# Batch 0's opening rearranged: a preload in 16 transfers, A normalised in two parts, the vote's values in PSUM, first w1 in fewer transfers

## The chip, the cores and the metric

One program on one core of a Trainium2 chip. The metric is the device time of one execution in microseconds. Three runs of the kernel before took 450.25, 451.38 and 451.59 us; their median, 451.38 us, is the time to beat.

## What is computed

Two stages in one program, with B=8 batches, H=8 heads, S=576 tokens, D=64; the model width is 512, there are E=8 experts of F=1024.

```python
# attention with 32 landmarks (means over 18 tokens), per batch and head
A  = softmax(q @ k_lm.T / 8)      # 576 x 32
Bm = softmax(q_lm @ k_lm.T / 8)   # 32 x 32
C  = softmax(q_lm @ k.T / 8)      # 32 x 576
Z  = Bm.T / (norm1(Bm) * norminf(Bm) + 1e-6)
for _ in range(6): Z = 2 * Z - Z @ Bm @ Z
x  = A @ Z @ C @ v                # heads side by side: 576 x 512
# every softmax divides by (sum + 1e-9)

# mixture of experts: one expert e for each token
logits = x @ w_gate; gate = sigmoid(x @ w_local)
e   = argmax(logits[s]) if s == 0 or gate[s] < 0.5 else e of token s-1
out = softmax(logits)[e] * (relu(x @ w1[e]) @ w2[e])
```

## The kernel before

The kernel never forms x. For each batch it makes A (softmax over 32 landmarks) and a small matrix W = Z C v, so that x W1 = A (W W1). Each batch is given to one expert, that of most of its tokens; tokens of other experts are gathered and treated in a slot at the end. For a batch, `mm1` makes the hidden layer from A and G = W·w1 in three products of high and low halves, and `after` multiplies it with w2, again in high and low halves (`split_w2` on ScalarE and GpSimd). Eight f-blocks and two passes over the tokens make 16 steps; the small work of the next batches is threaded between these steps by times that are written out (`at_time`, `STEADY`). This part is one long stream of matmuls.

The order inside each engine is that in which the program issues instructions (`manual_schedule`). Before the stream stands `startup`, by hand, for batch 0:

- SyncE's queue issues every load: q and k of batch 0, v, q and k of batch 1, and `firsts` (L945), the first quarter of w1's f-blocks' first block for all eight experts (2 MB), since the expert is not known yet.
- `max_c`, `exp_c`, `norms` and six Newton steps (`newton`, `newton_add`) run on VectorE and TensorE; `ez` holds their state. `c_v_rows` accumulates C v in the PSUM tile `pv`; `u` is pv divided by C's sums, `pw` and `wc` carry it through Z, `newton_wt` turns it, and `newton_gate` makes the gate's weights `wgc`.
- A stands in `sa` in two head groups g=0 and 1: row maxima (`sa_max`, VectorE and a subtraction on GpSimd), `sa_exp` (ScalarE), `sa_sum` (VectorE), `sa_norm` (epsilon and reciprocal on VectorE, product on GpSimd), `sa_back` (a transposition on VectorE into `full`).
- `gates` multiplies `full` with `wgc` (L825), `gate_rows` turns the result (L833), and `vote` (L859) picks batch 0's expert into a register that SyncE and TensorE load (L1226).
- Then `load_w1` and `get_w2` issue the expert's weights; `first_w1` uses `firsts`, `second_block` uses w1's second block (`w_w1` with L1247, its halves split by `split_g`, L1266 and L1269) and has the score products of batch 1 (`c_products`, `c_max`) between. `fresh` (L839) makes the token choices.
- `keep_busy` and the loops at L189, L191 and L1174 are matmuls whose result nobody reads. `lq0`, `lk0`, `lq2`, `lk2` are pieces of batch 1's landmark sums.

A tile's PSUM or SBUF buffer is reused in turn; a transfer waits for the one eight transfers before it on the queue, as there are eight semaphores in rotation.

Of the kernel before, what the change touches and what calls it, by code (L numbers as in the profile page):

```python
# [24 lines left out]
P = 128  # L25
# [38 lines left out]
def nystrom_attn_then_sticky_moe(ctx, tc, qT, kT, v, wg, w12, out):  # L64
# [123 lines left out]
    pz = one.tile([P, 512])  # L188
    for _ in range(11):  # L189
        nc.tensor.matmul(pz, zeros[:, 0:P], zeros, start=True, stop=True)  # L190
    for _ in range(18):  # L191
        nc.tensor.matmul(pz[:, 0:16], zeros[:, 0:P], zeros[:, 0:16], start=True, stop=True)
# [419 lines left out]

    def c_products(st, k0, n):


        out, x = (st["pc"][1], 0) if k0 == 512 else (st["pc"][0], k0)
        for c in range(4):
            for g in range(2):
                h = head(g, c)
                r = slice(64 * (h % 2), 64 * (h % 2) + 64)  # L620
                nc.tensor.matmul(out[g][32 * c:32 * c + 32, x:x + n], st["ql"][r, h // 2, :],
                                 st["k"][r, h // 2, k0:k0 + n], start=True, stop=True)
# [216 lines left out]
    def fresh(st):  # L839

        lg8 = st["lg"][:, :, 0:E]
        mx = st.get("mx")
        if mx is None:
            mx = sm.tile([P, NBLK], F32, name="mxl")
            nc.vector.reduce_max(out=mx, in_=lg8, axis=AX.X)
        pe = st["pe"] = sm.tile([P, NBLK, E], F32, name="pe")
        nc.vector.tensor_tensor(out=pe, in0=lg8, in1=mx.unsqueeze(2).broadcast_to([P, NBLK, E]), op=ALU.subtract)
        eq = sm.tile([P, NBLK, E], F32, name="eq")
        nc.vector.scalar_tensor_tensor(out=eq, in0=pe, scalar=0.0, in1=keys, op0=ALU.is_ge, op1=ALU.mult)
        fr = sm.tile([P, NBLK], F32, name="fr")  # L850
        nc.vector.tensor_tensor(out=fr, in0=st["lg"][:, :, E], in1=bound, op=ALU.is_le)
        am = sm.tile([P, NBLK], F32, name="am")
        nc.vector.reduce_max(out=am, in_=eq, axis=AX.X)
        d1 = st["d1"] = wide[:, 0:NBLK]
        nc.vector.tensor_mul(d1, fr, am)
        yield 0.5
        nc.scalar.activation(out=pe, in_=pe, func=AF.Exp)

    def vote(st, between):  # L859


        lg8 = st["lg"][:, :, 0:E]
        mx = st["mx"] = sm.tile([P, NBLK], F32, name="mxl")
        nc.vector.reduce_max(out=mx, in_=lg8, axis=AX.X)
        pick = sm.tile([P, E, NBLK], BF16, name="ohb")
        nc.vector.tensor_tensor(out=pick, in0=lg8.rearrange("p k e -> p e k"), in1=mx.unsqueeze(1).broadcast_to([P, E, NBLK]),
                                op=ALU.is_equal)
        pt = one.tile([P, E])
# [4 lines left out]
        best = sm.tile([P, 1], I32, name="best")  # L873
        nc.vector.tensor_reduce(out=best, in_=pt, axis=AX.X, op=ALU.min)
        nc.vector.tensor_single_scalar(regs[:, 0:1], best, 15, op=ALU.bitwise_and)
# [57 lines left out]
    def startup(st, nx):  # L933
# [10 lines left out]
        firsts = pre.tile([P, E, 512], F32, name="w1f")  # L944
        nc.sync.dma_start(out=firsts, in_=w12[:, 0, :, 0:512].rearrange("e p x -> p e x"))  # L945
        sc = sm.tile([P, 2, 3], F32, name="sc0", bufs=1)
# [119 lines left out]
        full = st["full"] = at.tile([P, 2, S], F32, name="at")  # L1066

        def sa_max(g):
            nc.vector.reduce_max(out=mxa[:, g], in_=sa[:, g], axis=AX.X)
            nc.gpsimd.tensor_tensor(out=sa[:, g], in0=sa[:, g], in1=mxa[:, g].unsqueeze(2).broadcast_to([P, NJ, M]),  # L1070
                                    op=ALU.subtract)

        def sa_exp(g):
            nc.scalar.activation(out=sa[:, g], in_=sa[:, g], func=AF.Exp, scale=scale)

        def sa_sum(g):
            nc.vector.reduce_sum(out=rsa[:, g], in_=sa[:, g], axis=AX.X)

        def sa_norm(g):
            inverse(rsa[:, g], 1e-9)  # L1080
            nc.gpsimd.tensor_tensor(out=sa[:, g], in0=sa[:, g], in1=rsa[:, g].unsqueeze(2).broadcast_to([P, NJ, M]), op=ALU.mult)

        def sa_back(g):
            nc.vector.transpose(out=full[:, g], in_=sa[:, g].rearrange("p j l -> p (j l)"))

# [22 lines left out]
        newton(4)  # L1108
        sa_max(1)
        c_v_rows(st, pv, 0, range(3, 5))  # L1110
        c_v_rows(st, pv, 1, range(0, 2))
        sa_exp(0)
        sa_sum(0)
        newton_add(4)
        newton(5)
        nc.vector.reduce_sum(out=sums[:, 2:4], in_=sc, axis=AX.X)
        nc.vector.reciprocal(out=sums[:, 2:4], in_=sums[:, 2:4])
        c_v_rows(st, pv, 1, range(2, 5))
        idle = ph.tile([P, 512], F32, name="ph")
        keep_busy(3, idle)  # L1120
        lq2_half(0)
        sa_norm(0)
        newton_add(5)
        sa_exp(1)
        u = st["u"] = sm.tile([P, 2, D], F32, name="u")
        for g in range(2):
            nc.scalar.mul(out=u[:, g], in_=pv[:, g], mul=sums[:, 2 + g:3 + g])
        sa_sum(1)
        sa_norm(1)
        lq2_half(1)  # L1130
        sa_back(0)
        lk0(0)
        pw = ph.tile([P, 2, D], F32, name="ph")
# [3 lines left out]
        for g in range(2):  # L1137
            nc.scalar.mul(out=wc[:, g], in_=pw[:, g].unsqueeze(1).broadcast_to([P, 2, D]), mul=st["rc"][:, g:g + 1])
        one.banks = ((ph, "ph"),)
        at_once(newton_wt(0, st))  # L1140
# [9 lines left out]
        a_high(0)  # L1150
        a_low(0)
        for g in range(2):
            for q in range(2):
                r, x = slice(64 * q, 64 * q + 64), slice(M * (q ^ g), M * (q ^ g) + M)
                src, dst = st["wt"][r, g, x], wts[r, g, 0, x]
                nc.scalar.copy(out=replace(dst, ap=(dst.ap[0], (P + 2 * M, 2), (1, M))),
                               in_=replace(src, ap=(src.ap[0], (2 * M, 2), (1, M))))
        idle = ph.tile([P, 512], F32, name="ph")
        keep_busy(1, idle)
        lq0(1)  # L1160
        newton_gate(0, st)
        keep_busy(2, idle)
        sa_back(1)
        a_high(1)
        nc.sync.dma_start(out=ad[0:P * 2 * NJ].rearrange("(p x) l -> p x l", p=P), in_=sa.rearrange("p g j l -> p (g j) l"))
        lk0(1)
        one.banks = ((pg, "pg"),)
# [5 lines left out]
        pz = one.tile([P, 512])  # L1173
        for _ in range(22):  # L1174
            nc.tensor.matmul(pz[:, 0:16], ones, ones[:, 0:16], start=True, stop=True)

        e = st["e"] = expert_of(regs[0:1, 0:1], (ET.SP, ET.PE))
        st["w1", 0] = load_w1(e, 0, ((nc.sync, 1, 1, 0, P), (nc.sync, 2, 1, 0, P), (nc.sync, 3, 1, 0, P)))
        get_w2(0, 0)
        get_w2(0, 1)  # L1180
        st["w1", 1] = load_w1(e, 1, ((nc.sync, 0, 2, 0, P), (nc.sync, 2, 2, 0, P)))
        get_w2(0, 2)
# [6 lines left out]
        lq0(1)  # L1189
        lq0(1)  # L1190
        lq2(0)
# [5 lines left out]
        def second_block():  # L1197
            c_begin(nx, (one, one))
            c_begin_rest(nx, (one, Banks((pg, "pg"))))
            c_products(nx, 0, 512)  # L1200
            lk2(0)
            lk2(1)
            g1 = w_w1(st, 0, 1, 1, ((py, "py"), (py, "py")))
            next(g1)
            c_products(nx, 512, 96)
            c_max(nx, 1, (0,))
# [633 lines left out]
```

## Time and profile before

| | |
|---|---|
| median of 3 runs | 451.38 us (450.25 to 451.59) |
| the profiled execution's own time | 451.21 us |
| its span in the profile | 449.4 us |
| TensorE busy | 435.1 us, 97% |
| VectorE, ScalarE, GpSimd busy | 63%, 48%, 43% |

The span runs from the first to the last instruction, and 1.8 us of the execution lie outside it. PE is TensorE, PEld its weight loads, DVE VectorE, ACT ScalarE, POOL GpSimd, SP SyncE; a q behind a name is that engine's sequencer. L12 is line 12 of the kernel before. A matmul of 32-bit floats appears as two matmuls and two weight loads.

### The profile page before, as it was taken

The page shows a single profiled execution, that of the slowest core. Times are in us where ns is not written, and L with a number is a line of the kernel's source. Part 1 is how long each engine was busy: PE and PEld are TensorE (multiplying, and loading weights), DVE is VectorE, ACT ScalarE, POOL GpSimd, SP SyncE. Part 2 cuts the span into 40 slices and gives each one's busy share as a digit, 9 for nine tenths or more (in the row PEclk, how much of TensorE's full clock was granted, in tenths as well). Part 3 has the DMA queues.
Part 4 walks back from the last instruction along what each step waited for, and adds up shares of the span by engine and source line. Part 5 has one row for each costly group of instructions (what it writes and reads, how often), then busy time and mean ns, then how long its engine had stood idle before and what let it go on. Part 6 is the DMA issues. An engine that isn't in the chain of part 4 may idle for free.

```text
span 449.4 us, 12512 instructions
## 1 busy us (share of the span) xinstructions
PE 435.1 (97%) x4898; PEld 337.1 (75%) x4898; DVE 284.5 (63%) x869; ACT 216.0 (48%) x577; POOL 192.0 (43%) x235
## 2 busy tenths in 40 slices
PE   8888999999999999999999999999999999999996
PEld 3455777777786788878887788788887778776885
DVE  7878786666858576665766574656555786954111
ACT  2546525467354751566253752465145414445611
POOL 5456663165815664263632650174116601055520
PEclk9999999999999999999999999999999999999999
DMA  8959952779569697649957615831164315692211
GB/s 303 378 198 350 367 190 98 268 287 261 210 160 382 202 388 159 245 164 341 290 138 260 237 54 125 318 110 48 55 233 158 113 44 173 252 313 95 97 31 50
DMA packets 62365, 91.53 MB, mean 204 GB/s; under 512 B 26731, under 2 KB 28267, under 8 KB 61152
## 3 DMA queue, kind: packets, MB, share of 16 engines
q1 hardware_dynamic: 60960, 86.23, 57.0%
q0 software_dynamic: 1344, 4.48, 2.7%
q8 instruction: 39, 0.64, 0.6%
q14 instruction: 22, 0.18, 0.1%
HBM read 75.27 MB, written 15.47 MB: 202 GB/s over the span
## 4 chain that ended last, share of the span: by engine, by line
PE 77%; DVE 13%; ACT 5%; issue 2%; DMA 1%; POOL 1%; SPq 0%; DVEq 0%; ACTq 0%; POOLq 0%
PE py L1337 33%; PE ph L1295 19%; PE pg L1346 5%; PE ph L1247 2%; PE one L416 2%; PE one L463 1%; DVE h L1307 1%; PE one L562 1%; PE py L1573 1%; DMA k_t<-kT 1%; PE one L517 1%; DVE gl L1269 1%; PE one L825 1%; POOL t L265 1%; DVE sk L261 1%
## 5 line engine op out<-in xcount | busy, mean ns | idle before, releaser
L1337 PE MATMUL py<-wh,h 128*128 128x512 f32 x504 | 161.6, 403 | 0.1
L1284 POOL TENSOR_TENSOR wl<-raw,wh 128x512 fp32r<-128x512 f32 x64 | 82.2, 1293 | 70.8 <-ACT wh L1282 69.7
L1302 ACT ACTIVATE h<-ph 128x256 fp32r<-128x256 f32 (+1 forms) x128 | 52.4, 413 | 111.2 <-PE ph L1295 94.2
L1337 PEld LDWEIGHTS py<-wh,h 128*128 128x128 f32 x504 | 86.4, 189 | 25.2 <-issue 13.2
L1307 DVE SCALAR_TENSOR_TENSOR h<-ph,h 128x256 fp32r<-128x256 f32 x128 | 53.0, 416 | 61.0 <-ACT h L1302 58.2
L1337 PE MATMUL py<-wl,h 128*128 128x512 f32 x252 | 80.5, 400 | 0.0
L1295 PE MATMUL ph<-ath,gh 128*128 128x320 f32 (+1 forms) x256 | 77.5, 303 | 1.5 <-ACT gh L1266 0.8
L1295 PE MATMUL ph<-ath,gl 128*128 128x320 f32 (+1 forms) x256 | 75.8, 296 | 0.0
L1295 PE MATMUL ph<-atl,gh 128*128 128x320 f32 (+1 forms) x256 | 75.6, 295 | 0.0
L1295 PEld LDWEIGHTS ph<-ath,gh 128*128 128x128 f32 x256 | 48.4, 189 | 9.1 <-ACT h L1302 2.2
L1337 PEld LDWEIGHTS py<-wl,h 128*128 128x128 f32 x252 | 45.9, 188 | 11.6 <-issue 1.3
L1295 PEld LDWEIGHTS ph<-atl,gh 128*128 128x128 f32 x256 | 48.3, 189 | 3.9
L1295 PEld LDWEIGHTS ph<-ath,gl 128*128 128x128 f32 x256 | 48.3, 189 | 0.2 <-DVE gl L1269 0.2
L1282 ACT CAST wh<-raw 128x512 fp32r<-128x512 f32 x69 | 43.2, 627 | 2.2 <-DMA raw<-w 1.4
L1406 POOL TENSOR_TENSOR ys<-ys,yl 64x512 f32<-64x512 f32 x8 | 10.3, 1281 | 58.5 <-ACT yl L1404 58.5
L265 POOL TENSOR_TENSOR t<-q_t 128x288 f32<-128x288 f32 x20 | 14.5, 747 | 23.5 <-DVE sk L267 23.5
L423 DVE TENSOR_TENSOR et<-et,one 128x64 f32<-128x64 f32 x36 | 7.9, 220 | 24.7 <-ACT et L422 16.4
L794 POOL TENSOR_TENSOR sa<-sa,rsa 128x1152 f32<-128x1152 f32 x7 | 14.9, 2133 | 19.9 <-DVE s L693 13.2
L265 POOL TENSOR_TENSOR t<-k_t 128x288 f32<-128x288 f32 x22 | 17.0, 795 | 11.9 <-DVE sq L267 10.8
L1346 PE MATMUL pg<-wl,h 128*128 128x512 f32 x56 | 21.9, 391 | 0.0
L1346 PE MATMUL pg<-wh,h 128*128 128x512 f32 x56 | 21.8, 390 | 0.0
L1395 ACT ACTIVATE ys<-py,token 128x512 f32<-128x512 f32 x30 | 19.0, 685 | 5.0 <-PE py L1337 4.7
(435 smaller groups left out, 729.3 us busy)
## 6 DMA issues: line engine op xcount, KB each, us to landing
raw<-w SPq DMA_DIRECT2D x75, 256.0 KB
raw<-w SPq DMA_DIRECT2D x16, 1024.0 KB
k_t<-kT SPq DMA_DIRECT2D x9, 1152.0 KB
q_t<-qT SPq DMA_DIRECT2D x9, 1152.0 KB
out<-ys SPq DMA_DIRECT2D x31, 256.0 KB
v_t<-v SPq DMA_DIRECT2D x20, 256.0 KB
ad<-sa POOLq DMA_DIRECT2D x7, 576.0 KB, 3.1
v_t<-v SPq DMA_DIRECT2D x3, 1024.0 KB
```

Of the source, the lines that this page charges most:

```text
L265: nc.gpsimd.tensor_add(t9[:, i], src[:, a + i, :, 0:9], src[:, a + i, :, 9:18])
L416: return {1: lambda: each_place(lambda g, r: nc.tensor.matmul(pn[r, g, :], et[r, g, 0:32], et[r, g, n0:64], start=True, stop=True))}, part ...
L794: nc.gpsimd.tensor_tensor(out=sa, in0=sa, in1=rs.unsqueeze(2).broadcast_to([P, 2 * NJ, M]), op=ALU.mult)
L1282: by(out=wh, in_=raw)
L1284: rest.tensor_tensor(out=wl, in0=raw, in1=wh.bitcast(F32), op=ALU.subtract)
L1295: mm = nc.tensor.matmul(hp, w[:, g, c], x[:, g, s0:s0 + n], start=(i == 0), stop=(i == 5))
L1302: nc.scalar.activation(out=h[:, 0:e], in_=hp[:, 0:e], func=AF.Relu)
L1307: nc.vector.scalar_tensor_tensor(out=h[:, 384:384 + m], in0=hp[:, 0:m], scalar=0.0, in1=h[:, 0:m].bitcast(F32), op0=ALU.max, op1=ALU.subtract)
L1337: nc.tensor.matmul(yps[k], h[:, part + i * P:part + i * P + P], w, start=(f == 0 and part == 0 and w is wh), stop=(f == NC2 - 1 and part = ...
L1346: nc.tensor.matmul(yps[4], hs[ff][1], w, start=(ff == 0 and w is w2[ff][0]), stop=(ff == NC2 - 1 and w is w2[ff][1]))
L1395: nc.scalar.mul(out=ys, in_=yp, mul=st["pw"][:, k:k + 1])
L1406: nc.gpsimd.tensor_tensor(out=ys[0:64], in0=ys[0:64], in1=yl[0:64], op=ALU.add)
```

## The change

- The preload of `firsts` becomes 16 transfers of 64 rows each (128 KB), in place of one of 2 MB. One matmul that reads 16 columns of `firsts` replaces one of the 22 small ones after the vote.
- In the softmax of A, the subtraction and the product on GpSimd, the exponential, the sum and the transposition of group 1 come in two parts of 9 token blocks; the epsilon is added by ScalarE (`sa_eps`), and the reciprocal stands alone on VectorE. `u` is one VectorE instruction in place of two on ScalarE. C's sums, `newton_add(4)` and several landmark pieces change their places.
- `vote` and `own` keep maxima, totals and the best key in PSUM; `fresh` computes the maxima again.
- The first w1 blocks come in one transfer each for block 1, blocks 2 and 3, and the second half, in place of five. In `second_block` the first score products are halved around `w_w1`, and those of the last 96 columns come after the next `w_w1`.
- The warm-up has 12 wide and 17 small matmuls, in place of 11 and 18.

```diff
-    for _ in range(11):
+    for _ in range(12):
...
-    for _ in range(18):
+    for _ in range(17):
...
     def vote(st, between):
-        mx = st["mx"] = sm.tile([P, NBLK], F32, name="mxl")
+        ps = one.tile([P, 512])
+        pt, mx, best = ps[:, 0:E], ps[:, 16:16 + NBLK], ps[:, 32:33].bitcast(I32)
...
-        nc.sync.dma_start(out=firsts, in_=w12[:, 0, :, 0:512].rearrange("e p x -> p e x"))
+        for i in range(E):
+            for r in (slice(0, 64), slice(64, P)):
+                nc.sync.dma_start(out=firsts[r, i], in_=w12[i, 0, r, 0:512])
...
+        whole, first, second = slice(0, NJ), slice(0, 9), slice(9, NJ)
+        def sa_eps(g):
+            nc.scalar.activation(out=rsa[:, g], in_=rsa[:, g], func=AF.Identity, bias=least)
...
         sa_max(1)
+        sa_scaled(mxa, 1, first, ALU.subtract)
+        sa_scaled(mxa, 1, second, ALU.subtract)
+        sa_exp(0)
         c_v_rows(st, pv, 0, range(3, 5))
         c_v_rows(st, pv, 1, range(0, 2))
-        sa_exp(0)
-        sa_sum(0)
         newton_add(4)
         newton(5)
+        sa_sum(0)
+        sa_exp(1, first)
+        sa_eps(0)
         c_v_rows(st, pv, 1, range(2, 5))
-        keep_busy(3, idle)
-        lq2_half(0)
-        sa_norm(0)
+        keep_busy(2, idle)
         newton_add(5)
-        sa_exp(1)
-        for g in range(2):
-            nc.scalar.mul(out=u[:, g], in_=pv[:, g], mul=sums[:, 2 + g:3 + g])
-        sa_sum(1)
-        sa_norm(1)
-        lq2_half(1)
-        sa_back(0)
-        lk0(0)
+        nc.vector.tensor_tensor(out=u, in0=pv, in1=sums[:, 2:4]..., op=ALU.mult)
+        nc.vector.reciprocal(out=rsa[:, 0], in_=rsa[:, 0])
+        sa_scaled(rsa, 0, whole, ALU.mult)
+        sa_exp(1, second)
+        sa_sum(1, first)
+        sa_sum(1, second)
...
+        sa_eps(1)
+        nc.vector.reciprocal(out=rsa[:, 1], in_=rsa[:, 1])
+        sa_scaled(rsa, 1, first, ALU.mult)
+        sa_scaled(rsa, 1, second, ALU.mult)
+        sa_back(0)
...
-        lq0(1)
+        sa_back(1, first)
         newton_gate(0, st)
         keep_busy(2, idle)
-        sa_back(1)
+        sa_back(1, second)
+        lk0(0)
+        lk0(1)
         a_high(1)
...
+        nc.tensor.matmul(pz[:, 0:16], ident, firsts[:, :, 0:2], start=True, stop=True)
...
-        st["w1", 0] = load_w1(e, 0, ((nc.sync, 1, 1, 0, P), (nc.sync, 2, 1, 0, P), (nc.sync, 3, 1, 0, P)))
+        st["w1", 0] = load_w1(e, 0, ((nc.sync, 1, 1, 0, P), (nc.sync, 2, 2, 0, P)))
...
-        st["w1", 1] = load_w1(e, 1, ((nc.sync, 0, 2, 0, P), (nc.sync, 2, 2, 0, P)))
+        st["w1", 1] = load_w1(e, 1)
...
         lq0(1)
-        lq0(1)
+        lq0(2)
...
-            c_products(nx, 0, 512)
+            c_products(nx, 0, 512, (0, 1))
             lk2(0)
             lk2(1)
             g1 = w_w1(st, 0, 1, 1, ((py, "py"), (py, "py")))
             next(g1)
-            c_products(nx, 512, 96)
+            c_products(nx, 0, 512, (2, 3))
             c_max(nx, 1, (0,))
             at_once(g1)
...
+        at_time(1.007, c_products, nx, 512, 96)
```

## Rows read from the trace of the kernel before

**Rows 1.** The page: span, PE's busy time and count, the queue that brings instructions.
```profile
span 449.4 us, 12512 instructions
PE 435.1 (97%) x4898; PEld 337.1 (75%) x4898; DVE 284.5 (63%) x869; ACT 216.0 (48%) x577; POOL 192.0 (43%) x235
q8 instruction: 39, 0.64, 0.6%
```
**Rows 2.** Busy time by stretch: us, each engine's busy time and count, clock, DMA, GB/s.
```profile
100.00:200.00 100.00, 99.16 (x1282) 78.63 (x1280) 67.59 (x205) 52.92 (x146) 51.48 (x54) 1.00 0.76 242
```
**Rows 3.** Chain of waits of the first 45 us: start, us, what.
```profile
25.51 0.46 issue
```
**Rows 4.** DMA queues from 16.6 to 23.2 us: packets, MB, share of 16 engines.
```profile
q1 hardware_dynamic: 1292, 2.54, 104.2%
```
**Rows 5.** DMA queues from 23.2 to 25 us.
```profile
q8 instruction: 1, 0.02, 4.8%
```
**Rows 6.** Timeline, 20 to 27 us: start, us, engine, line, operation, [idle before <- releaser].
```profile
20.37 0.28 DVE L1062 TENSOR_TENSOR yl<-ph,yl 128x128 f32<-128x128 f32 x1
...
20.71 0.33 PE L1055 MATMUL ph<-yl 32*32 32x32 f32 x16 [0.51 <-DVE yl L1062]
...
21.66 0.50 ACT L1127 ACTIVATE u<-pg,sums 128x64 f32<-128x64 f32 x2
...
22.20 0.42 PE L1134 MATMUL ph<-u,yl 32*32 32x64 f32 x16
...
22.69 0.62 ACT L1138 ACTIVATE wc<-ph,rc 128x128 f32<-128x128 f32 x2 [0.53 <-PE ph L1134]
...
22.92 0.27 DVE L177 RECIPROCAL rsa<-rsa 128x18 f32<-128x18 f32 x1
...
23.32 1.16 POOL L1081 TENSOR_TENSOR sa<-sa,rsa 128x576 f32<-128x576 f32 x1 [0.47 <-ACT wc L1138]
...
24.64 0.18 DVE L760 COPY wgc<-ph 128x18 f32<-128x18 f32 x1
...
24.74 0.77 DVE L1084 STREAM_TRANSPOSE at<-sa 128x576 f32<-128x576 f32 x1
...
25.96 0.52 PE L825 MATMUL pg<-at,wgc 128*32 128x128 f32 x10 [0.46 <-issue]
...
26.69 0.35 DVE L833 STREAM_TRANSPOSE lg<-pg 128x160 f32<-128x160 f32 x1 [0.85 <-PE pg L832]
```
**Rows 7.** One line of GpSimd, the product of the later batches: ns min/median/max.
```profile
L794 POOL TENSOR_TENSOR sa<-sa,rsa x7: 2128/2133/2136, 57.2 to 354.9; 128x1152 f32<-128x1152 f32 x7
```
**Rows 8.** Timeline, 5 to 8 us.
```profile
5.90 0.65 PE L192 MATMUL one<-sa 128*128 128x16 bf16 x18
...
7.24 0.46 DVE L977 TENSOR_REDUCE nm<-one 128x1 f32<-128x288 f32 x1
```
**Rows 9.** Timeline of SyncE's DMA issues, 4 to 35 us.
```profile
5.01 0.62 SPq L244 DMA_DIRECT2D v_t<-v  x1
...
10.25 0.59 SPq L945 DMA_DIRECT2D w1f<-w  x1
...
29.00 1.43 SPq L1232 DMA_DIRECT2D raw<-w  x3
```
**Rows 10.** What SyncE's queue waited for, up to 60 us: us in total, times, longest.
```profile
SPq L751 <- DMA v_t<-v: 2.0, 1, 2.0
```
**Rows 11.** Timeline, 30 to 41 us.
```profile
32.39 0.18 PEld L1247 LDWEIGHTS py<-raw,wt 64*32 64x32 f32 x16 [0.75 <-DMA raw<-w]
...
32.64 0.69 DVE L631 TENSOR_REDUCE nm8c<-one 128x1 f32<-128x512 f32 x1 [0.86 <-PE one L621]
...
39.94 0.59 PE L1247 MATMUL ph<-raw,wt 64*32 64x512 f32 x1 [0.97 <-DVE atl L1310]
```
**Rows 12.** One line of VectorE, in `fresh`: ns min/median/max, first and last start.
```profile
L849 DVE SCALAR_TENSOR_TENSOR eq<-pe,keys x8: 199/201/1344, 37.6 to 367.3; 128x40 f32<-128x40 f32 x8
```
**Rows 13.** One line of VectorE, in `own`.
```profile
L904 DVE TENSOR_TENSOR tot<-tot,ranks x7: 166/167/169, 79.2 to 373.3; 128x8 f32<-128x8 f32 x7
```

More of the change, by code (lines that the diff above doesn't have):

```diff
@@ L165, in nystrom_attn_then_sticky_moe @@
     nc.gpsimd.memset(small, 1e-6)
+    least = const.tile([P, 1], F32, name="least")
+    nc.gpsimd.memset(least, 1e-9)
     psa = ctx.enter_context(tc.tile_pool(name="psa", bufs=3, space=PSUM))
@@ L611, in c_begin_rest, with c_products @@
         st["pc"][1].extend(x.tile([P, 512])[:, 0:96] for x in banks)
-    def c_products(st, k0, n):
+    def c_products(st, k0, n, places=range(4)):
         out, x = (st["pc"][1], 0) if k0 == 512 else (st["pc"][0], k0)
-        for c in range(4):
+        for c in places:
             for g in range(2):
@@ L841, in fresh @@
         lg8 = st["lg"][:, :, 0:E]
[L842 to L845, printed above, removed]
+        mx = sm.tile([P, NBLK], F32, name="mxl")
+        nc.vector.reduce_max(out=mx, in_=lg8, axis=AX.X)
         pe = st["pe"] = sm.tile([P, NBLK, E], F32, name="pe")
@@ L867, in vote @@
                                 op=ALU.is_equal)
-        pt = one.tile([P, E])
         for k in range(NBLK):
@@ L896, in own @@
     def own(b, st):
-        best = sm.tile([P, 1], I32, name="best")
-        ps = one.tile([P, E, NBLK])
+        bank = one.tile([P, 512])
+        ps = bank[:, 0:E * NBLK].rearrange("p (e k) -> p e k", k=NBLK)
+        pt, best = bank[:, 128:128 + E], bank[:, 256:257].bitcast(I32)
         nc.tensor.matmul(ps, counts[:, 0], st["ohb"], start=True, stop=True)
-        pt = sm.tile([P, E], F32, name="tot")
         nc.vector.reduce_sum(out=pt, in_=ps, axis=AX.X)
@@ L1066, in startup, with sa_scaled, sa_exp, sa_sum @@
         full = st["full"] = at.tile([P, 2, S], F32, name="at")
+        whole, first, second = slice(0, NJ), slice(0, 9), slice(9, NJ)
         def sa_max(g):
             nc.vector.reduce_max(out=mxa[:, g], in_=sa[:, g], axis=AX.X)
[L1070 to L1084, printed above, removed]
+        def sa_scaled(x, g, j, op):
+            nc.gpsimd.tensor_tensor(out=sa[:, g, j], in0=sa[:, g, j],
+                                    in1=x[:, g, j].unsqueeze(2).broadcast_to([P, j.stop - j.start, M]), op=op)
+        def sa_exp(g, j=whole):
+            nc.scalar.activation(out=sa[:, g, j], in_=sa[:, g, j], func=AF.Exp, scale=scale)
+        def sa_sum(g, j=whole):
+            nc.vector.reduce_sum(out=rsa[:, g, j], in_=sa[:, g, j], axis=AX.X)
+        def sa_eps(g):
+            nc.scalar.activation(out=rsa[:, g], in_=rsa[:, g], func=AF.Identity, bias=least)
+        def sa_back(g, j=whole):
+            nc.vector.transpose(out=full[:, g, M * j.start:M * j.stop], in_=sa[:, g, j].rearrange("p j l -> p (j l)"))
         lq0 = landmark_parts(nx, "q", 0)
@@ L1093, in startup @@
         sa_max(0)
+        sa_scaled(mxa, 0, whole, ALU.subtract)
         lk0_half(0)
@@ L1101, in startup @@
         c_turn(4, 1)
+        nc.vector.reduce_sum(out=sums[:, 2:4], in_=sc, axis=AX.X)
+        nc.vector.reciprocal(out=sums[:, 2:4], in_=sums[:, 2:4])
         newton_add(2)
@@ L1109, in startup @@
         sa_max(1)
+        sa_scaled(mxa, 1, first, ALU.subtract)
+        sa_scaled(mxa, 1, second, ALU.subtract)
+        sa_exp(0)
         c_v_rows(st, pv, 0, range(3, 5))
         c_v_rows(st, pv, 1, range(0, 2))
-        sa_exp(0)
-        sa_sum(0)
         newton_add(4)
         newton(5)
-        nc.vector.reduce_sum(out=sums[:, 2:4], in_=sc, axis=AX.X)
-        nc.vector.reciprocal(out=sums[:, 2:4], in_=sums[:, 2:4])
+        sa_sum(0)
+        sa_exp(1, first)
+        sa_eps(0)
         c_v_rows(st, pv, 1, range(2, 5))
         idle = ph.tile([P, 512], F32, name="ph")
-        keep_busy(3, idle)
-        lq2_half(0)
-        sa_norm(0)
+        keep_busy(2, idle)
         newton_add(5)
-        sa_exp(1)
         u = st["u"] = sm.tile([P, 2, D], F32, name="u")
-        for g in range(2):
-            nc.scalar.mul(out=u[:, g], in_=pv[:, g], mul=sums[:, 2 + g:3 + g])
-        sa_sum(1)
-        sa_norm(1)
-        lq2_half(1)
-        sa_back(0)
-        lk0(0)
+        nc.vector.tensor_tensor(out=u, in0=pv, in1=sums[:, 2:4].unsqueeze(2).broadcast_to([P, 2, D]), op=ALU.mult)
+        nc.vector.reciprocal(out=rsa[:, 0], in_=rsa[:, 0])
[3 more added lines that the diff above has]
+        sa_sum(1, second)
         pw = ph.tile([P, 2, D], F32, name="ph")
@@ L1151, in startup @@
         a_low(0)
+        lq2_half(0)
+        lq2_half(1)
         for g in range(2):
@@ L1159, in startup @@
         keep_busy(1, idle)
-        lq0(1)
+        sa_back(1, first)
         newton_gate(0, st)
         keep_busy(2, idle)
-        sa_back(1)
+        sa_back(1, second)
+        lk0(0)
+        lk0(1)
         a_high(1)
         nc.sync.dma_start(out=ad[0:P * 2 * NJ].rearrange("(p x) l -> p x l", p=P), in_=sa.rearrange("p g j l -> p (g j) l"))
-        lk0(1)
         one.banks = ((pg, "pg"),)
@@ L1173, in startup @@
         pz = one.tile([P, 512])
-        for _ in range(22):
+        nc.tensor.matmul(pz[:, 0:16], ident, firsts[:, :, 0:2], start=True, stop=True)
+        for _ in range(21):
             nc.tensor.matmul(pz[:, 0:16], ones, ones[:, 0:16], start=True, stop=True)
         e = st["e"] = expert_of(regs[0:1, 0:1], (ET.SP, ET.PE))
-        st["w1", 0] = load_w1(e, 0, ((nc.sync, 1, 1, 0, P), (nc.sync, 2, 1, 0, P), (nc.sync, 3, 1, 0, P)))
+        st["w1", 0] = load_w1(e, 0, ((nc.sync, 1, 1, 0, P), (nc.sync, 2, 2, 0, P)))
         get_w2(0, 0)
         get_w2(0, 1)
-        st["w1", 1] = load_w1(e, 1, ((nc.sync, 0, 2, 0, P), (nc.sync, 2, 2, 0, P)))
+        st["w1", 1] = load_w1(e, 1)
         get_w2(0, 2)
```

1 line of the change is left out of this document (removed).

## The prediction

> **What bounds the kernel now.** I read the page first. TensorE is busy for 435.1 of 449.4 us [rows 1], but that is a mean over an opening of some 40 us and a stream. The busy times by stretch separate them: from 100 to 200 us TensorE works 99.16 of 100 us [rows 2], so an edit there can give back well under 1 us in a hundred, while every microsecond by which the stream begins earlier should arrive at the end unchanged. The stream begins when batch 0's expert is known. So I followed the chain of waits back from the choice. It runs through the turning of the gate's results at 26.69 us [rows 6], and before that through the gate's matmuls, whose second group starts at 25.96 us. What it waited for, the second half of `full`, had ended at 24.74 + 0.77 = 25.51 us, and the chain names the 0.46 us between as issue: no semaphore explains it [rows 3, 6].
>
> What was late there is, I think, code. The instruction queue moved 39 packets, 0.64 MB, so 16 KB each, and TensorE has 2 x 4898 matmuls and weight loads: 251 to a packet, so these packets are TensorE's program [rows 1]. From 16.6 to 23.2 us none of them moved, while the load queue held the engines at 104% [rows 4]; one moved right after 23.2 us, when the preload was nearly through [rows 5]. TensorE came to a stop in the middle of a group of matmuls 2 us later. Preload and code compete for the same engines, and the 2 MB transfer seems to have held the packet back.
>
> **The change, part by part.** All times are on the trace of before (span 449.4 us; the execution took 451.21 us, 0.17 us under the median of 451.38, to which the result is put).
>
> *The gate's weights.* Now `newton_add(4)` stands behind `sa_sum(0)` and runs at 20.37 us, and the next Newton matmul has waited 0.51 us for it at 20.71 [rows 6]. Moved ahead of the sum it lets that matmul go at 20.2. The products behind it and `pv` follow 0.5 earlier, and `u` is one VectorE operation of 128x128, 0.28 us by its neighbour at 20.37, in place of 0.50 us on ScalarE (21.66). So `pw` starts at 21.4 and not at 22.20. `wc` follows 0.8 earlier than 22.69, and `wgc` could be there 0.75 earlier than 24.64; it stands behind the first half of `sa_back(1)` and is done at 24.4, not 24.82.
>
> *A's second group.* Its reciprocal is at 22.92 us [rows 6]. In the new order ScalarE adds the epsilon behind `wc`, at 22.5, and the reciprocal ends at 23.0 in place of 23.2. The product on GpSimd is 1.16 us for 576 elements [rows 6] and 2.13 for 1152 [rows 7]: 0.19 fixed and 1.69 ns an element, so 0.67 for each half. They run from 23.15 to 24.45, no earlier than the whole one that ended at 23.32 + 1.16 = 24.48. The gain is in what comes behind: before, VectorE was busy with other pieces until 24.74 and then turned all of A in 0.77; now only the second half is left, about 0.42 by the same row, from 24.5 to 24.9. That is 25.51 - 24.9 = 0.6 us earlier. The landmark pieces `lk0`, moved behind it, fit into the 0.85 us for which VectorE waits for the gate's matmuls (26.69).
>
> *The preload.* Sixteen transfers, of which eight can be under way: the transfer behind the preload waited 2.0 us for v's, eight before it [rows 10]. An issue of 64 rows took 0.62 us at 5.01 [rows 9]. The second eight therefore go out from about 21 to 25.5 us, and the last lands 1.6 to 3.4 us later (3.4 is the first w1 block, issued at 29.00 and used at 32.39 [rows 9, 11]): 27.0 to 28.9, near 27.4. The read of all 16 columns, in TensorE's program before the choice, needs it at about 27.6. Cost: 0 to 1.3, I take 0.1, as the transfers behind a busy queue land sooner than the one from rest. The store of A, behind them, may still run when the first w1 block starts: 0 to 0.3, I take 0.1. In return the code packet finds gaps between small transfers, and the 0.46 us goes: 0 to 0.46, I take all of it.
>
> The Trainium skill, DMA: Bandwidth & Descriptors (Rules for kernel authors), speaks against the split: coalesce small transfers, and don't cut one into partition halves. By its fixed cost of about 2 us a transfer two rounds of eight would end 4 us after the first goes out, sooner than my issue times allow, so the sum would stay. Its section on queues says that an engine changes between rings only at packet ends, up to 64 descriptors; the rows of the code packet agree with a long hold, and no run here shows its length.
>
> *Warm-up.* The 18 small matmuls start at 5.90, 0.65 us in all; the first maximum on VectorE at 7.24 follows its matmuls at once [rows 8]. One more matmul of 512 columns is 0.2 us at the rate of the later ones, 0.43 at the early rate. VectorE is dense here, so this passes to the choice. 0 to 0.4; I take 0.2.
>
> *Vote in PSUM, `own`, `fresh`.* The operations are as many, and in PSUM they can't be held by GpSimd, as `eq` was once: 1344 ns where 199 is usual [rows 12]. In `vote` GpSimd was idle, so 0 to 0.1; in `own` the addition never took over 169 ns [rows 13]: 0. `fresh` has one maximum more, 0.2 us, just before `eq`; while `eq` is blocked to the same end by GpSimd it costs nothing, else 0.2 to 0.3.
>
> *After the choice.* Two fewer issues of 0.48 us [rows 9] free SyncE, but the bytes are the same, and TensorE waited 0.75 us for the first block [rows 11]: nothing gained before it lands. Halving the score products puts `c_max` (0.69 at 32.64) before the low half of G and its matmuls behind `w_w1`: 0.6 us later for the second `mm1`. It is covered by the 0.97 us for which TensorE waits at 39.94 for VectorE [rows 11]; without that cover it costs 0.6. The other way, if VectorE gets there sooner, up to 0.8 of the same gap comes back. I take 0.
>
> The sum: -0.6 (A) - 0.4 (code; the gate's matmuls cannot start before `wgc`) + 0.2 (warm-up) + 0.1 + 0.1 (preload) = -0.6 us. On the median: 450.8.
>
> **The rivals.** *The stop at 25.5 stays.* Then 0.4 of the gain goes: -0.2, 451.2 us. For it: only one such stop shows, and its cause was read from what was late. The Trainium skill, Runtime: NRT & Kernel Launch (Instruction fetch mechanics), says crossing a 16 KB block is mostly hidden; by that rule this is the case that comes. The trace's 0.46 us without a semaphore speaks against it.
>
> *The preload lands late.* One mechanism on the slower side: from 27.6 us on, each microsecond of delay in the last of the 16 transfers is one in TensorE's program, as the read of `firsts` stands ahead of the choice; at 28.3 the gain is used up, and at 28.9, my upper bound, the time is -0.7 + 1.3 = +0.6: 452.0. For it: 0.62 us an issue. Against it: TensorE has 0.1 of slack before w1 lands, and the preload of before was drained by 24.
>
> *The new order in `second_block` shows.* If TensorE's 0.97 us doesn't cover it, +0.6 and up to 0.3 for `fresh`: +0.3, 451.7.
>
> *The gap at 39.94 closes too.* Half of it or more returns: -1.4, 450.0.
>
> **How the numbers follow.** Chances: forecast 0.42, stop stays 0.18, late preload 0.14, order shows 0.10, gap closes 0.16. A measurement of this kernel tells 0.3% from no change, about 1.35 us. Faster by more needs the last case and half of its spread, or a forecast that is 0.8 too small: 0.25. Slower by more is the late preload beyond its bound, or two bad cases at once: 0.12. Within: 0.63. The range, 449.8 to 451.8, holds the gap case and nearly the late preload; the forecast's own is 450.2 to 451.4.
>
> **What would show it.** In the changed trace: no issue of 0.4 us within the gate's matmuls and a code packet between 20 and 23 us (else the first rival); the turning of the gate's results near 26.0 in place of 26.69; no wait of the read of `firsts` (else the second); the matmuls of w1's second half 0.6 before 39.94. The forecast is wrong if the choice comes no earlier, or comes earlier and the stream doesn't.

## The result, and the profile of the changed kernel

The changed kernel takes 456.92 us (456.43 to 457.23, four runs) where the kernel before takes 451.16 (four runs, the three of the table above among them): a ratio of 1.0129 (95% interval 1.0111 to 1.0148). It is slower by 1.3%. The forecast was 450.8 us, the range ended at 451.8. The profiled execution took 457.23 us, the slowest of the four. Medians of the kernel before differ by 0.9 us from one set of runs to another (450.22 to 451.16), so versions are compared below by their ratio to the runs of it that were timed beside them.

The page of the changed kernel, for [rows 1]: as many matmuls, and a span 6.0 us longer.

```profile
span 455.4 us, 12531 instructions
PE 436.1 (96%) x4898; PEld 339.0 (74%) x4898; DVE 284.6 (63%) x870; ACT 216.3 (48%) x578; POOL 192.2 (42%) x238
```

The busy times by stretch, with the columns of [rows 2].

```profile
21.00:27.00 6.00, 5.35 (x74) 2.39 (x72) 5.07 (x18) 4.12 (x13) 5.20 (x7) 1.00 0.54 154
25.00:30.00 5.00, 2.29 (x25) 0.99 (x21) 3.65 (x12) 1.52 (x5) 5.00 (x7) 0.91 0.63 183
30.00:35.00 5.00, 3.51 (x33) 3.45 (x34) 0.29 (x1) 0.53 (x2) 0.05 (x1) 0.50 0.82 265
100.00:200.00 100.00, 99.09 (x1306) 78.72 (x1295) 67.51 (x207) 52.24 (x146) 52.16 (x58) 1.00 0.79 248
```

From 100 to 200 us the stream is as dense as before, so most of the time was lost ahead of it. How much, the line of `own` [rows 13] tells: it runs first at 84.4 us in place of 79.2, 5.2 us later.

```profile
L903 DVE TENSOR_TENSOR one<-one,ranks x7: 174/175/175, 84.4 to 379.5; 128x8 f32<-128x8 f32 x7
```

Its last run comes 6.2 us later (379.5 against 373.3). Of this further microsecond, 0.87 us is a stop within one group of matmuls, in the timeline:

```profile
213.79 0.20 PE L451 MATMUL one<-wg_sb,wt 64*32 64x9 f32 x2 [0.87 <-issue]
```

Twelve of the fourteen profiles kept here have such a stop between 207 and 216 us, of 0.6 to 0.9 us, that of the fastest version too; the profile of the kernel before has none. So it doesn't come from the preload's lateness, and the two spans differ by about 0.9 us more than that explains. Its cause is open.

From 25 to 30 us TensorE was busy for 2.29 of 5 us, where it was 4.31 before, and from 30 to 35 us its granted clock was 0.50, the 1.2 GHz level. From 21 to 27 us the DMA engines, which should have finished the preload, worked at 0.54 (0.76 before).

First what went as forecast. The timeline from 20.9 to 27 us, for [rows 6].

```profile
21.80 0.62 ACT L1143 ACTIVATE wc<-ph,rc 128x128 f32<-128x128 f32 x2 [0.24 <-PE ph L1139]
...
23.00 1.30 POOL L1075 TENSOR_TENSOR sa<-sa,rsa 128x288 f32<-128x288 f32 x2 [0.33 <-DVE rsa L1145]
...
24.34 0.48 DVE L1088 STREAM_TRANSPOSE at<-sa 128x288 f32<-128x288 f32 x1
...
24.40 0.94 PE L827 MATMUL pg<-at,wgc 128*32 128x160 f32 x16 [0.17 <-POOL sa L1075]
...
25.45 0.35 DVE L835 STREAM_TRANSPOSE lg<-pg 128x160 f32<-128x160 f32 x1
...
26.90 0.16 DVE L874 TENSOR_SCALAR regs<-one 128x1 int32<-128x1 int32 x1
```

A's second half is turned by 24.82 (forecast 24.9). The 16 matmuls of the gate run without a stop, and the choice is there at 26.90 us, 1.22 earlier than in the kernel before. Its choice and its `first_w1`, in the timeline:

```profile
28.12 0.15 DVE L875 TENSOR_SCALAR regs<-best 128x1 int32<-128x1 int32 x1
...
29.31 1.13 PE L1257 MATMUL py<-w1f,ys 128*128 x8 [0.24 <-ACT ql L275]
```

Then what did not. SyncE's issues in the timeline, for [rows 9]:

```profile
9.95 18.87 SPq L946 DMA_DIRECT2D w1f<-w  x16
28.94 0.51 SPq L753 DMA_DIRECT2D wtd<-wt  x1
29.56 0.36 SPq L1179 DMA_DIRECT2D ad<-sa  x1
30.68 0.95 SPq L1247 DMA_DIRECT2D raw<-w  x2
```

The preload's line by itself, with the columns of [rows 7] (ns min/median/max, first and last start in us):

```profile
L946 SPq DMA_DIRECT2D w1f<-w x16: 465/595/1397, 10.0 to 28.2; - x16
```

And what the queue waited for, up to 32 us, with the columns of [rows 10]:

```profile
SPq L946 <- DMA k_t<-kT: 3.1, 2, 2.1
SPq L946 <- DMA v_t<-v: 2.8, 2, 2.6
SPq L946 <- DMA q_t<-qT: 2.1, 2, 1.4
```

The sixteen issues hold SyncE from 9.95 to 28.8 us, where the single one took 0.59: 8.0 us of it are six waits, one each ahead of the second to the seventh, for loads that were issued earlier; the rest is issuing. The seventh goes out at 21.06 us. From there on the queue waits for nothing: ten issues follow one another in 7.76 us, the ninth at 23.01, the last at 28.23. The two stores stand behind them (24.24 and 24.70 before), and the first w1 load goes out at 30.68, not 29.00, although the choice is earlier. TensorE in the same stretch:

```profile
26.50 0.81 PE L929 MATMUL one<-ones 128*128 128x512 bf16 x3
31.39 0.58 PE L1187 MATMUL one<-w1f,ident 128*128 128x16 f32 x2 [4.08 <-DMA wtd<-wt]
...
32.62 2.07 PE L1272 MATMUL py<-w1f,ys 128*128 x8
...
45.05 0.59 PE L1262 MATMUL ph<-raw,wt 64*32 64x512 f32 x1 [1.11 <-issue]
```

The read of `firsts` waits 4.08 us. The profile names the store of `wtd`, the last landing in that gap, but the instruction reads only `ident` and `firsts`: what it waits for is the preload, whose last transfer was issued at 28.2 us. `first_w1` then starts at 32.62, 3.3 us later than before (29.31), and takes 2.07 us in place of 1.13. w1's second half waits 1.11 us, where it waited 0.97 before, and comes 5.1 us after the 39.94 of [rows 11].

### The profile page after: what moved, and what is told of

Same layout as the page of the kernel before. It is cut to its first block, busy times and chain, and to the rows that moved or that the text cites. A ratio compares the mean times of both kernels' runs of the same rounds, so it can differ in the third digit from the quotient of the medians.

```text
span 455.4 us, 12531 instructions
## 1 busy us (share of the span) xinstructions
PE 436.1 (96%) x4898; PEld 339.0 (74%) x4898; DVE 284.6 (63%) x870; ACT 216.3 (48%) x578; POOL 192.2 (42%) x238
## 4 chain that ended last, share of the span: by engine, by line
PE 77%; DVE 12%; ACT 5%; issue 2%; DMA 2%; POOL 1%; SPq 0%; DVEq 0%; ACTq 0%; POOLq 0%
PE py L1352 33%; PE ph L1310 19%; PE pg L1361 5%; PE ph L1262 2%; PE one L418 2%; PE one L465 1%; PE one L564 1%; DVE h L1322 1%; PE py L1588 1%; DMA k_t<-kT 1%; PE one L519 1%; PE one L827 1%; POOL t L267 1%; DVE gl L1284 1%; PE ph L1567 1%
## 5 line engine op out<-in xcount | busy, mean ns | idle before, releaser
L1421 POOL TENSOR_TENSOR ys<-ys,yl 64x512 f32<-64x512 f32 x8 | 10.3, 1282 | 58.5 <-ACT yl L1419 58.5
```

What stands on the lines that cost most here:

```text
L1421: nc.gpsimd.tensor_tensor(out=ys[0:64], in0=ys[0:64], in1=yl[0:64], op=ALU.add)
```

## The experiments

The theory after the result: the preload's form is the whole loss, and the other edits are worth the gain forecast for them. Rivals: the loss is in the other edits; it needs the early read; it is SyncE's queue rather than the landing; it is the clock.

| version | ratio to before | 95% interval |
|---|---|---|
| changed kernel, first and second time | 1.0129, 1.0120 | 1.0111 to 1.0148, 1.0106 to 1.0135 |
| changed, preload in one transfer | 1.0013 | 0.9992 to 1.0034 |
| changed, four transfers of 128 rows | 1.0014 | 0.9998 to 1.0030 |
| changed, eight transfers of 128 rows | 0.9981 | 0.9965 to 0.9997 |
| the same, old order of `second_block` | 0.9997 | 0.9983 to 1.0011 |
| changed, sixteen of 128 rows x 256 columns | 1.0082 | 1.0069 to 1.0095 |
| changed, eight of 64 rows | 1.0082 | 1.0060 to 1.0104 |
| before, with sixteen of 64 rows alone | 1.0126 | 1.0094 to 1.0157 |
| before, with eight of 128 rows alone | 1.0002 | 0.9994 to 1.0011 |
| changed, no early read | 1.0110 | 1.0081 to 1.0140 |
| changed, expert's loads from ScalarE | 1.0143 | 1.0129 to 1.0158 |
| changed, TensorE kept busy to the read | 1.0130 | 1.0115 to 1.0145 |

**One transfer again.**

```diff
-        for i in range(E):
-            for r in (slice(0, 64), slice(64, P)):
-                nc.sync.dma_start(out=firsts[r, i], in_=w12[i, 0, r, 0:512])
+        nc.sync.dma_start(out=firsts, in_=w12[:, 0, :, 0:512].rearrange("e p x -> p e x"))
```

> The changed kernel with the preload as one 2 MB transfer again; everything else of the change stays, the early read of firsts too. Theory (the sixteen transfers are the loss, through their late landing at 31.05 us and the SyncE queue that they fill until 28.8): the expert's first w1 issue comes at 27.5 to 28 us, the read of firsts waits for nothing, TensorE's clock stays whole, and the time is 449.8 to 450.9 us, under the kernel before by 0.3 to 1.3; the upper end if the stop without a semaphore near 25 us is back because the code packet is held again. Rival (the loss is in the later edits: halved score products, w1 in fewer transfers, values in PSUM): the time stays at 455 to 457 us.

451.1 us, 0.2 above the theory's range. The loss is gone with this one edit, and the rival of the later edits with it. But no gain is left either. The gate's matmuls in the timeline show why:

```profile
24.73 0.47 PE L827 MATMUL pg<-at,wgc 128*32 128x160 f32 x7 [0.17 <-POOL sa L1073]
25.87 0.52 PE L827 MATMUL pg<-at,wgc 128*32 128x128 f32 x9 [0.67 <-issue]
```

The DMA queues from 23 to 24 us have the code packet (none moved from 16.6 to 23):

```profile
q8 instruction: 1, 0.02, 8.1%
```

The stop without a semaphore is back, 0.67 us, and the choice is at 27.94.

**The sixteen transfers alone, in the kernel before** (the same lines the other way round; no early read).

> The kernel before with the preload in sixteen transfers, and nothing else of the change: no early read of firsts, w1 in its five transfers, batch 0's A as before. Theory (lateness of the sixteen): first_w1 itself waits for the last landing at about 31 us, SyncE issues the expert's loads after the sixteen and two more, near 30.7 us, and the time is 455 to 458 us. Rival (the loss needs the early read or the fewer w1 transfers): 450.5 to 452 us.

456.03 us. One part of the change makes the whole loss. TensorE's two waits, at `first_w1` and at the first w1 block:

```profile
31.22 1.13 PE L1259 MATMUL py<-w1f,ys 128*128 x8 [2.28 <-DMA wtd<-wt]
...
36.05 0.45 PE L1249 MATMUL py<-raw,wt 64*32 64x128 f32 x16 [1.59 <-DMA raw<-w]
```

The second, against 32.39 in [rows 11], shows that the transfers behind the preload are late too. And here the granted clock stays whole, as the busy times show, with the same loss:

```profile
30.00:35.00 5.00, 3.24 (x30) 2.08 (x30) 1.75 (x5) 1.17 (x5) 1.14 (x2) 1.00 0.89 268
```

So the fallen clock is not needed for it.

**Without the early read.**

```diff
-        nc.tensor.matmul(pz[:, 0:16], ident, firsts[:, :, 0:2], start=True, stop=True)
-        for _ in range(21):
+        for _ in range(22):
```

> The changed kernel with its sixteen transfers, but without the read of all of firsts ahead of the choice; 22 small matmuls stand there as in the kernel before. Theory A (the late queue of SyncE is the loss): the loads of the expert still go out at about 30.7 us, first_w1 still waits for the preload to 31 us, and the time is 456 to 457.5 us, as the changed kernel. Theory B (the read holds TensorE's program up, and the clock falls behind it): TensorE comes to the choice at 27.6 us, and the time falls to 451 to 454 us.

455.59 us, 0.4 under theory A's range and 1.6 over theory B's. The wait moves to `first_w1` itself, which needs the same bytes:

```profile
32.84 2.04 PE L1271 MATMUL py<-w1f,ys 128*128 x8 [4.79 <-DMA wtd<-wt]
```

The fall that theory B forecast is not there. Whether the early read has a cost of its own can't be told: 1.0110 against 1.0129 and 1.0120, intervals that overlap.

**Eight transfers of 128 rows.**

```diff
-            for r in (slice(0, 64), slice(64, P)):
-                nc.sync.dma_start(out=firsts[r, i], in_=w12[i, 0, r, 0:512])
+            nc.sync.dma_start(out=firsts[:, i], in_=w12[i, 0, :, 0:512])
```

> The changed kernel with the preload in eight transfers of 128 rows, one for each expert, in place of sixteen of 64 rows. Theory (what counts is how many transfers SyncE issues, at 0.5 to 0.64 us each and not over eight under way): the issues end by 19 to 23 us, the last lands by 26 us, the read of firsts does not wait, and the time is 450 to 451.2 us. Rival (small transfers move slowly beside the rest, however many): landing near 29 us or later, time 453 to 456.5 us.

449.54 us, 0.5 under the theory's range: the fastest version and under both kernels. The gain over the kernel before is 0.03 to 0.35%, an interval that only just leaves out zero. The line of its preload:

```profile
L945 SPq DMA_DIRECT2D w1f<-w x8: 327/328/585, 10.1 to 20.5; - x8
```

Its busy times from 21 to 27 us:

```profile
21.00:27.00 6.00, 5.37 (x73) 2.37 (x72) 5.06 (x17) 4.17 (x13) 5.20 (x7) 1.00 0.87 318
```

TensorE in its timeline:

```profile
27.22 0.29 PE L1186 MATMUL one<-w1f,ident 128*128 128x16 f32 x2
...
28.21 1.15 PE L1271 MATMUL py<-w1f,ys 128*128 x8 [0.18 <-issue]
...
38.99 0.59 PE L1261 MATMUL ph<-raw,wt 64*32 64x512 f32 x1
```

The last issue goes out at 20.5 us in place of 28.2, the engines move 318 GB/s in place of 154, the read waits for nothing, and w1's second half comes 0.95 us before the 39.94 of the kernel before.

**Sixteen of 128 rows, and eight of 64 rows**: the two halves of the difference.

```diff
 sixteen_wide
+            for x in (slice(0, 256), slice(256, 512)):
+                nc.sync.dma_start(out=firsts[:, i, x], in_=w12[i, 0, :, x])
 eight_narrow
+        for i in range(0, E, 2):
+            for r in (slice(0, 64), slice(64, P)):
+                nc.sync.dma_start(out=firsts[r, i:i + 2], in_=w12[i:i + 2, 0, r, 0:512].rearrange("e p x -> p e x"))
```

> The changed kernel with sixteen transfers still, but each of 128 rows by 256 columns in place of 64 rows by 512 columns: the same bytes, the same number. Theory A (what hurts is the 64-row form, whose issue SyncE holds for 0.60 us where one of 128 rows took 0.33): the second eight go out in 8 x 0.37 = 3 us, from 22 to 25 us, the last lands at 26.5 to 27.5 us, the read of firsts waits 0 to 0.3 us, and the time is 449.5 to 450.8 us. Theory B (what hurts is the count of sixteen, with eight of them held until the first eight have landed): the last lands at 29 us or later, and the time is 453 to 456.5 us.

> The changed kernel with eight transfers, each of 64 rows and two experts (256 KB, as in the version of eight with 128 rows). Theory A (the 64-row form is the cost, whatever the count): issues of 0.47 us, paced by landings as far as 21.5 us, so all are out before the second round that hurts; only the transfers themselves can be slower, and the time is 449.5 to 451 us, the same as with 128 rows, if the issue time was the only harm; 452 to 455 us if 64-row transfers also move slowly. Theory B (the count is the cost): 449.5 to 450 us.

453.74 and 453.91 us. The first lies in the range of theory B (the count), the second in the upper branch of theory A (64-row transfers that also move slowly). Neither theory had both: each half costs about 0.8%, and the two together 1.2%. The sixteen wide ones: the preload's line, the busy times, the read.

```profile
L946 SPq DMA_DIRECT2D w1f<-w x16: 328/430/1207, 9.6 to 25.6; - x16
```

```profile
21.00:27.00 6.00, 5.35 (x77) 2.36 (x74) 5.00 (x16) 4.31 (x14) 5.20 (x7) 1.00 0.66 199
```

```profile
28.84 0.37 PE L1187 MATMUL one<-w1f,ident 128*128 128x16 f32 x2 [1.35 <-DMA wtd<-wt]
```

The eight narrow ones, the same three views:

```profile
L946 SPq DMA_DIRECT2D w1f<-w x8: 595/596/1362, 10.3 to 23.7; - x8
```

```profile
21.00:27.00 6.00, 4.36 (x83) 1.97 (x73) 4.00 (x14) 4.57 (x14) 5.20 (x7) 1.00 0.96 226
```

```profile
26.33 0.52 PE L827 MATMUL pg<-at,wgc 128*32 128x128 f32 x9 [1.02 <-issue]
...
30.66 0.37 PE L1187 MATMUL one<-w1f,ident 128*128 128x16 f32 x2 [1.86 <-DMA wtd<-wt]
```

They fail in different ways. Sixteen wide ones leave the engines idle: share 0.66, with the last issue at 25.6 us. Eight narrow ones keep them busy, at 0.96, but move 226 GB/s where the eight wide ones moved 318 at 0.87: divided by the share, 235 against 366. The two versions with sixteen lie between: 285 for the changed kernel and 302 for the wide ones. The narrow ones also bring the stop in the gate's matmuls back, 1.02 us. The wide ones have rows of 1 KB, not 2 KB, and each narrow one spans two experts, so whether the cost is that of the number, the size or the form is left open. In both, `first_w1` took as long as in the changed kernel (2.05 and 2.07 us).

**The expert's loads from ScalarE's queue** (w1 and the first two of w2).

```diff
-        e = st["e"] = expert_of(regs[0:1, 0:1], (ET.SP, ET.PE))
-        st["w1", 0] = load_w1(e, 0, ((nc.sync, 1, 1, 0, P), (nc.sync, 2, 2, 0, P)))
...
+        e = st["e"] = expert_of(regs[0:1, 0:1], (ET.SP, ET.PE, ET.Activation))
+        st["w1", 0] = load_w1(e, 0, ((nc.scalar, 1, 1, 0, P), (nc.scalar, 2, 2, 0, P)))
+        get_w2(0, 0, nc.scalar)
+        get_w2(0, 1, nc.scalar)
+        st["w1", 1] = load_w1(e, 1, ((nc.scalar, 0, 4, 0, P),))
...
```

> The changed kernel with its sixteen transfers; the expert's first w1 and w2 loads (five issues) go from ScalarE's queue, which is not behind the preload, in place of SyncE's. Theory A (the late queue of SyncE is what the expert's loads pay): the w1 issue comes at 27.3 us in place of 30.68, w1 lands with or before the preload, and the time falls by 2 to 4 us, to 453 to 455. Theory B (the late landing of the preload, which TensorE must read first, sets the time): the read of firsts still waits to about 31 us or longer, and the time stays at 455.5 to 457.5 us.

456.81 us: theory B. ScalarE's issues and TensorE's read, in the timeline:

```profile
27.80 1.44 ACTq L1247 DMA_DIRECT2D raw<-w  x2
...
32.43 0.58 PE L1187 MATMUL one<-w1f,ident 128*128 128x16 f32 x2 [5.10 <-DMA wtd<-wt]
```

The loads go out 2.9 us earlier, and the read of the preload starts 1.04 us later. SyncE's late queue alone is not the loss.

**TensorE kept busy up to the read** (`keep_busy(19)` for `keep_busy(3)`), and the changed kernel once more.

> The changed kernel with 16 more keep_busy matmuls of 512 columns (about 3.4 us) ahead of the read of firsts, which fill TensorE's wait from 27.3 to 31.4 us. Theory (the granted clock of 0.50 from 29.1 to 35.9 us came from that idle time): the clock stays whole, first_w1 takes 1.15 in place of 2.07 us, and the time falls by 0.7 to 1.2 us, to 455.6 to 456.3. Rival (the chain behind is set by landings, and the clock cost nothing): 456.6 to 457.2 us.

> The changed kernel itself once more, timed beside the other three on one chip, so that the run with TensorE kept busy ahead of its read (ratio 1.0130 to the kernel before) has a partner of more rounds. If the fallen clock costs what its trace shows (first_w1 2.07 in place of 1.15 us and the matmuls behind it), the ratio here is 1.0145 to 1.016; if the cost is taken up by the later waits, 1.012 to 1.0135.

455.8 us (1.0130) and 455.67 (1.0120). With TensorE busy, the clock stays whole, as the busy times show:

```profile
30.00:35.00 5.00, 4.38 (x47) 3.17 (x48) 1.19 (x4) 0.62 (x3) 0.41 (x1) 1.00 0.96 287
```

The read and `first_w1` in the same run's timeline:

```profile
31.22 0.37 PE L1187 MATMUL one<-w1f,ident 128*128 128x16 f32 x2
...
32.62 1.15 PE L1272 MATMUL py<-w1f,ys 128*128 x8 [0.51 <-issue]
```

So the fall to 0.50 came with the 4 us of idle time, and `first_w1` is 0.92 us shorter without it. The time doesn't follow: 455.8 us lies in the theory's range, but that was set against 456.92 us of other runs, and between the ratios nothing can be told. Later waits take up part of the gain: w1's second half starts at 44.60 with a wait of 1.44 us ahead of it, where the two profiles of the changed kernel have 45.05 with 1.11 and 45.36 with 0.49.

**The old order of `second_block`, with eight transfers.**

```diff
-            c_products(nx, 0, 512, (0, 1))
+            c_products(nx, 0, 512)
...
-            c_products(nx, 0, 512, (2, 3))
+            c_products(nx, 512, 96)
...
-        at_time(1.007, c_products, nx, 512, 96)
```

> Eight transfers of 128 rows, with second_block in the order of the kernel before: all the score products of 512 columns first, those of 96 columns ahead of the maximum. Theory (the new order delays the second mm1 by about 0.6 to 1 us and the wait for VectorE at w1's second half takes it up, so it costs nothing): the second mm1 comes 0.6 to 1 us earlier, that wait is back with 0.6 to 1.1 us, and the time is 449.3 to 450 us, as with the new order. Rival (the new order costs): 448.4 to 449 us. Other rival (the new order closed the gap and is worth its 0.97 us): 450.2 to 450.8.

449.92 us, in the theory's range; ratio 0.9997 against 0.9981, intervals that overlap. Its trace has the wait of [rows 11] again, where the new order has none:

```profile
39.17 0.59 PE L1260 MATMUL ph<-raw,wt 64*32 64x512 f32 x1 [1.20 <-DVE atl L1323]
```

What VectorE was late with is `eq`, the line of [rows 12], here with the old order:

```profile
L849 DVE SCALAR_TENSOR_TENSOR eq<-pe,keys x8: 199/201/1336, 36.8 to 367.4; 128x40 f32<-128x40 f32 x8
```

And with the new order, both with eight transfers:

```profile
L849 DVE SCALAR_TENSOR_TENSOR eq<-pe,keys x8: 199/200/202, 37.8 to 367.1; 128x40 f32<-128x40 f32 x8
```

1336 ns against 199 to 202. In the old order's timeline GpSimd splits w2 from the very time at which `eq` starts, 36.8 us, and to its end:

```profile
36.83 1.29 POOL L1297 TENSOR_TENSOR wl<-raw,wh 128x512 fp32r<-128x512 f32 x1
```

TensorE waits for what stands behind `eq`. The new order misses that by starting the third mm1 at 35.56 us and not at 34.56. In these two traces, then, the order costs 1 us and saves 1.2, but only while it keeps `eq` clear of GpSimd; the times don't tell the two orders apart. In the two profiles of the changed kernel `eq` took 1282 ns and 199, the wait at w1's second half 1.11 us and 0.49: it changes from one execution to the next. Nor is it always `eq`: with four transfers, in the new order, it was the operation that makes `wide`, 1.05 us for some 0.17, beside GpSimd's next split, and TensorE waited 1.45 us.

```profile
39.30 1.05 DVE L855 TENSOR_TENSOR wide<-fr,am 128x5 f32<-128x5 f32 x1
```

**Four transfers** (two experts each, 128 rows), and **eight alone in the kernel before**.

> The changed kernel with the preload in four transfers of 128 rows, two experts each (512 KB). Theory (the code packet passes between transfers, and no second round of issues exists): no stop without a semaphore among the gate's matmuls, last landing near 26 us, 449.2 to 450 us. Rival (larger transfers hold the code packet as the one of 2 MB did): the stop of 0.4 to 0.7 us is back, and the time is 450 to 451 us.

> The kernel before with the preload in eight transfers of 128 rows and nothing else of the change. Theory (the preload's form and the edits of A are two gains that add up): the stop of 0.46 us at 25.5 goes, the choice comes 0.3 to 0.5 us earlier than 28.12, and the time is 449.7 to 450.1 us where the kernel before has 450.3, half way to the version of eight with all the edits. Rival (the early choice buys nothing unless w1 also comes in fewer transfers): 450.2 to 450.6. Other rival (the edits of A are worth nothing): 449.3 to 449.6, as with all the edits.

450.28 and 450.27 us (1.0014 and 1.0002). Four behave as the rival said: a stop of 0.49 us in the gate's matmuls (and their executions spread widely, 449.5 to 453.0 us). Eight alone are the first rival, no gain: the stop is gone and the choice is at 27.89, 0.23 earlier (the theory had 0.3 to 0.5), but `first_w1` waits longer for `ql` of ScalarE (0.24 before). The row of four, then the one of eight alone:

```profile
25.48 0.52 PE L827 MATMUL pg<-at,wgc 128*32 128x128 f32 x9 [0.49 <-issue]
```

```profile
29.39 1.13 PE L1258 MATMUL py<-w1f,ys 128*128 x8 [0.56 <-ACT ql L275]
```

## Why the prediction was wrong, point by point

*The preload: the step that failed.* The landing of the last transfer was put near 27.4 us, and its cost at 0.1 us, at most 1.3. The read got it at 31.39, 4.0 us later. Three parts of the term were too small. The second eight were to start at about 21 us; the ninth went out at 23.01. What set that was not the landing of the first eight: behind the seventh issue no wait shows. It was the first seven, held until the loads ahead had landed (the three rows of waits), and then the issuing itself. The issues from the ninth to the last were to take 4.5 us and took 5.2: the price of 0.62 us an issue held (median 0.595), but one issue among them took 1.34 us. And the landing behind the last issue, priced at 1.6 to 3.4 us and taken near the lower end, took 3.2. For the 1.6 the prediction names no row, and no run shows it: the shortest landing of a preload transfer in the runs with sixteen is 2.6 us. Nor does a run show its reason, that transfers behind a busy queue land sooner than one from rest; here the queue was not busy, at a share of 0.54.

The Trainium skill, DMA: Bandwidth & Descriptors (Rules for kernel authors), which the prediction set against the split, says not to cut a transfer into partition halves. The traces agree: eight transfers of 256 KB moved 226 GB/s in halves and 318 with all 128 rows.

*The rival "the preload lands late"* had the mechanism: from 27.6 us each microsecond is one in TensorE's program. By its slope a landing at 31.39 is -0.7 + 3.8 = +3.1 us, and `first_w1` is 3.3 later. At w1's second half it is 5.1. The 1.8 between were not priced: 0.94 us of `first_w1` at the lower clock, 0.72 in the matmuls from its end to the wait (9.25 us in place of 8.53; the lower clock and the new order are both in it), and 0.14 in the wait itself, which the later mm1 should have shortened (`eq` took 1282 ns there). The runs don't give each of these a price of its own: with the clock whole, the wait was 1.44. The rival's upper end, 452.0 us, was too low, and the range stopped short even of that; the doubt about the bound had no place in it.

*A, the gate's weights.* Right: the reciprocal, the two products, the turning and `wc` stand within 0.16 us of the times worked out. The turning of the gate's results was better than forecast, 25.45 us in place of 26.0, and the choice with it.

*The code.* The stop goes with sixteen and with eight wide transfers, and stays with one, four and eight narrow ones. In the versions with the stop the packet of the instruction queue moved after 23 us, as in [rows 5]; in all others, the changed kernel among them, before. That the packet is what TensorE waits for is still inferred from this order; nothing here delayed the packet alone. Its worth was over-read, though: with eight transfers alone the earlier choice gave nothing, because `ql` was late next. It counts only where the other edits move the work ahead of `ql` too. That only one such stop shows, on which the rival of the stop leaned, holds for the profile of the kernel before alone: the changed kernel has one ahead of 213.79 us.

*The sum without the preload's loss* was -0.6 - 0.4 + 0.2 = -0.8 us. The version with eight transfers measures -0.73 against its own runs of the kernel before. With an interval of -0.1 to -1.6 us that is no proof of the terms, and the choice came 1.14 us earlier there, where the terms give 0.8; so the closeness is partly luck. The warm-up term was too high: the first maximum on VectorE moved by 0.08 us, from 7.24 to 7.32, and the choice does not show it.

*`second_block`.* The forecast was 0.6 us later, covered by the wait of 0.97. With eight transfers it was over 1.0 later (34.43 against 33.42), and the cover is a coincidence of VectorE with GpSimd that comes and goes with the times of w2's loads. There the wait was gone and w1's second half came no later (38.99 against 39.17); in the changed kernel's first profile the delay and the wait stood one behind the other. This is the third rival, hidden under the second.

## What to carry to other kernels

Time the split alone first: here it cost 1.3% by itself with sixteen pieces of 64 rows, and gave nothing with eight of 128. A transfer split into pieces is priced by its last landing, and that has three terms that a profile of the unsplit version doesn't show: when the queue lets the first pieces out, the issue time times the number, and whether the pieces in flight still fill the engines. In this kernel the pieces that did no harm kept all 128 partitions, and the queue had sent the last of eight at 20.5 us, 2.4 us before the next work for it was ready. Give the case in which every piece waits a place in the range.

## What was unexpected of the hardware

An issue of 64 rows of one expert holds SyncE for 0.465 us behind a wait and 0.595 behind another issue; one of 128 rows took 0.328, and 0.430 behind another in the version of sixteen. At 256 KB it was 0.596 (64 rows, two experts) against 0.328 (128 rows, one expert). In the versions with sixteen the longest single issue took 1.02 to 1.81 us. Eight transfers of 64 rows moved 226 GB/s with the engines busy at 0.96. TensorE's granted clock fell to 0.50 in a wait of 4.08 us, yet in this place the 0.92 us that it cost in `first_w1` could not be found in the kernel's time. And one small operation of VectorE, 199 ns alone and 1336 beside GpSimd's, can make TensorE wait for a microsecond at w1's second half.
